# One level of Strassen in the second feed-forward product, on one core of Trainium2

The kernel runs on one core of a Trainium2 chip. The metric is the device time of one execution in microseconds. Every kernel below was run beside the kernel before on the same chip. All runs quoted are fast: none is over 1.5% above the fastest run of its kernel.

## The reference

Four batches go through linear attention and then through a feed-forward block behind a Fourier mixing. Cut to what matters:

```python
# q, k, v: (4, 8, 768, 64); w_ch1: (512, 2048); w_ch2: (2048, 512)
for t in range(S):                      # per head: decaying state
    state = gamma * state + outer(k[t], v[t])
    y[t] = scale * q[t] @ state
x = y as (4, 768, 512)
u = x + real(fft(fft(x, axis=1), axis=2))
un = (u - mean(u)) / sqrt(var(u) + 1e-6)           # per row of 512
out = u + maximum(un @ w_ch1, 0) @ w_ch2
```

Per batch, 768 rows of 512 go through two products, 512 to 2048 and 2048 to 512. The kernel multiplies in 16-bit floats and adds up in 32 bits.

## The kernel before

A scheduler merges streams of units by a position that each is given (`emit`). The main stream is the feed-forward work of batch b. The attention and the mixing of batch b+1 are mixed into it, so every engine has one queue in which both kinds of work alternate, and it works through this queue in order.

```python
inp = pool("inp", 11)                      # buffers for q, k, v in 32 bits
ps_g = pool("ps_g", 5, space=PSUM)         # attention and mixing
ps_pm = pool("ps_pm", 3, space=PSUM)       # the two feed-forward products

def h_unit(b, rt, fb):                     # first product, 384 rows, 128 hidden columns
    psh = ps_pm.tile([P, 384], ...)
    for cb in range(4):
        nc.tensor.matmul(psh, w116[:, cb, fb*P:(fb+1)*P], unT[:, cb, rt*384:(rt+1)*384], ...)
    if fb in ACT_ROWS[...]:                # 8 to 10 of 16 on ScalarE
        nc.scalar.activation(ht16[:, fb, :], psh, AF.Relu, bias=0.0, scale=-1.0)
    else:                                  # the others on VectorE
        nc.vector.tensor_scalar(out=ht16[:, fb, :], in0=psh, scalar1=-1.0, scalar2=0.0,
                                op0=ALU.mult, op1=ALU.max)

def ch_unit(b, rt, rb3, part):             # second product, 128 rows, in 4 parts
    # ... a PSUM tile psc of 512 columns
    for fb in range(k0, k0 + NFB // n):
        nc.tensor.matmul(psc[:, c0:c1], ht16[:, fb, rb3*P:(rb3+1)*P], w216[:, fb, c0:c1], ...)
    if part % n == n - 1:
        nc.vector.scalar_tensor_tensor(out=ob[:, c0:c1], in0=psc[:, c0:c1], scalar=r,
                                       in1=u[:, rb, c0:c1], op0=ALU.mult, op1=ALU.add)
        nc.sync.dma_start(out[b, rb*P:(rb+1)*P, c0:c1], ob[:, c0:c1])
# ... batch 0 makes its first row tiles one at a time (h0_unit)
# feed-forward of a batch: 16 h_units, 3 x 4 ch_units, 16 h_units, 3 x 4 ch_units
```

## Time and profile before

| | before |
|---|---|
| time, median of 5 runs | 247.66 us (247.35 to 247.86) |
| span of the profiled run | 246.0 us |
| TensorE busy | 234.4 us |
| VectorE, ScalarE, GpSimd busy | 177.5, 124.3, 81.3 us |
| chain that ended last | 72% TensorE, 8% VectorE, 7% GpSimd |

Busy time says how long an engine had an instruction in work. The chain that ended last is the path from the last instruction back to the start, at each step to whatever released it. Here that path is nearly always TensorE's own previous instruction. The prediction shows the lines.

### The profile page before, as it was taken

How to read it: one execution, taken by the hardware profiler on the slowest of the kernel's cores; microseconds unless marked ns; L12 is line 12 of the kernel's file. 1: busy time of each engine (PE TensorE's matmuls, PEld its weight loads, DVE VectorE, ACT ScalarE, POOL GpSimd, SP SyncE). 2: the span in 40 equal slices, each digit the busy share in tenths (PEclk: the TensorE clock that was granted, in tenths of full speed). 3: DMA queues.
4: the chain of work that ended last, by engine and by line, in shares of the span. 5: the costliest groups of instructions: out<-in, count | busy, mean ns of one | idle time of the engine just before them, and what ended most of it. 6: DMA issues, size and time to landing. Idle time of an engine off the chain costs nothing.

```text
span 246.0 us, 5309 instructions
## 1 busy us (share of the span) xinstructions
PE 234.4 (95%) x2024; PEld 144.4 (59%) x2024; DVE 177.5 (72%) x430; ACT 124.3 (51%) x276; POOL 81.3 (33%) x146
## 2 busy tenths in 40 slices
PE   6897899999999999999999999999999998999994
PEld 2454668956676655665567446665666455445543
DVE  8998957898788788995987648887895657424122
ACT  8798669477785445742247415732257217202500
POOL 6667600376500068690001637660003214000000
PEclk9999999999999999999999999999999999999999
DMA  8998999699999287988999589596100331121012
GB/s 174 257 260 138 200 204 206 152 250 261 275 233 214 56 171 176 190 174 149 242 266 210 119 183 181 108 138 150 58 0 3 60 133 30 38 85 43 0 45 85
DMA packets 99209, 36.39 MB, mean 148 GB/s; under 512 B 89840, under 2 KB 96240, under 8 KB 99184
## 3 DMA queue, kind: packets, MB, share of 16 engines
q1 hardware_dynamic: 94960, 31.86, 62.5%
q0 software_dynamic: 4224, 4.19, 10.5%
q8 instruction: 16, 0.26, 0.5%
q14 instruction: 9, 0.07, 0.1%
HBM read 27.26 MB, written 6.29 MB: 136 GB/s over the span
## 4 chain that ended last, share of the span: by engine, by line
PE 72%; DVE 8%; POOL 7%; ACT 4%; SPq 3%; DMA 2%; issue 2%; POOLq 0%; DVEq 0%
PE psc L973 30%; PE psh L930 23%; SPq L159 3%; PE ps L730 3%; PE psh L947 3%; PE wkA L594 3%; DMA k<-in_k_dram 2%; PE wkY L648 2%; POOL u L864 2%; POOL u L866 2%; PE wkY L644 1%; DVE bst L883 1%; PE wkK L613 1%; DVE u L834 1%; PE pq L827 1%
## 5 line engine op out<-in xcount | busy, mean ns | idle before, releaser
L973 PE MATMUL psc<-w,ht 128*128 128x512 f16 (+1 forms) x400 | 89.6, 370 | 0.1
L930 PE MATMUL psh<-unT,w 128*128 128x384 f16 x448 | 81.3, 326 | 0.6 <-ACT ht L934 0.6
L973 PEld LDWEIGHTS <-ht 128*128 128x128 f16 x400 | 38.1, 98 | 35.5 <-issue 0.3
L930 PEld LDWEIGHTS <-w 128*128 128x128 f16 x448 | 42.3, 98 | 24.9 <-issue 1.3
L934 ACT ACTIVATE ht<-psh 128x384 f16<-128x384 f32 x64 | 30.6, 488 | 39.4 <-PE psh L930 38.3
L864 POOL TENSOR_TENSOR u<-u,x 128x256 f32<-128x256 f32 x21 | 13.3, 634 | 102.3 <-DVE u L834 90.7
L977 DVE SCALAR_TENSOR_TENSOR ob<-psc,stats,u 128x512 f32<-128x512 f32 (+1 forms) x25 | 18.1, 722 | 27.4 <-PE psc L973 27.3
L936 DVE TENSOR_SCALAR ht<-psh 128x384 f16<-128x384 f32 x48 | 26.3, 551 | 8.6 <-PE psh L930 8.3
L597 DVE TENSOR_TENSOR atm<-wkA,maskp 128x512 f16<-128x512 f32 x36 | 23.9, 685 | 1.0 <-PE wkA L594 1.0
L885 ACT ACTIVATE un<-u,stats 128x512 f16<-128x512 f32 x21 | 15.1, 721 | 16.9 <-DVE stats L884 8.7
L883 DVE BATCH_NORM_STATS2 bst<-u 128x6 f32<-128x512 f32 x21 | 14.6, 694 | 9.7 <-POOL u L866 9.5
L623 DVE SCALAR_TENSOR_TENSOR s<-s,gk,wkK 128x128 f16<-128x128 f16 x48 | 16.4, 343 | 2.3 <-ACT s L619 1.4
L656 ACT ACTIVATE x<-wkY,gexp 128x384 f16<-128x384 f32 x24 | 12.8, 580 | 9.3 <-PE wkY L648 9.3
L145 PE MATMUL wps<-ht 128*128 128x512 f16 x40 | 13.3, 439 | 2.2 <-POOL ht L196 2.2
L377 POOL TENSOR_SCALAR kd<-k,gexp 128x384 f16<-128x384 f32 x24 | 13.8, 584 | 2.4 <-DMA k<-in_k_dram 2.4
L866 POOL TENSOR_TENSOR u<-u,x 128x256 f32<-128x256 f32 x21 | 13.3, 634 | 2.8 <-DVE u L837 1.5
L594 PE MATMUL wkA<-qTz,kT 128*128 128x256 f16 x72 | 13.6, 273 | 0.0
L829 ACT COPY qn<-pq 128x128 f32<-128x128 f32 x18 | 4.9, 274 | 14.1 <-PE pq L827 13.9
L947 PE MATMUL psh<-unT,w 128*128 128x128 f16 x192 | 11.5, 219 | 0.1
L947 PEld LDWEIGHTS <-w 128*128 128x128 f16 x192 | 11.0, 98 | 0.7 <-issue 0.5
L382 POOL TENSOR_SCALAR v<-v 128x768 f16<-128x768 f32 x12 | 10.0, 830 | 2.0 <-DMA v<-in_v_dram 1.9
L594 PEld LDWEIGHTS <-kT 128*128 128x128 f16 x72 | 6.9, 98 | 6.0 <-DVE s L623 0.4
(164 smaller groups left out, 318.2 us busy)
## 6 DMA issues: line engine op xcount, KB each, us to landing
q<-in_q_dram SPq DMA_DIRECT2D x16, 384.0 KB, 6.2
k<-in_k_dram SPq DMA_DIRECT2D x16, 384.0 KB, 5.6
v<-in_v_dram SPq DMA_DIRECT2D x16, 384.0 KB, 6.6
out_dram<-ob SPq DMA_DIRECT2D x23, 256.0 KB, 2.6
w<-in_moe_w_ch_dram POOLq DMA_DIRECT2D x8, 512.0 KB, 11.1
out_dram<-ob SPq DMA_DIRECT2D x2, 128.0 KB, 1.7
unT<-un SPq DMA_TRANSPOSE x15, 2.4
qTz<-q16z SPq DMA_TRANSPOSE x8, 3.8
```

The lines of the kernel that those rows point to most:

```text
L594: mm = nc.tensor.matmul(wk[:, c2], st["kT"][:, c, :], st["qT"][:, :, c, :], start=True, stop=True)
L597: nc.vector.tensor_tensor(out=st["atm"][:, 2 * part:2 * part + 2], in0=wk, in1=maskp[:, PAIR_ORDER[i]].unsqueeze(1).to_broadcast([P, 2, 2, ...
L623: nc.vector.scalar_tensor_tensor(out=s16[:, c], in0=s16[:, c - 1], scalar=gk2[:, hp:hp + 1], in1=wk[:, c - c0], op0=ALU.mult, op1=ALU.add)
L864: nc.gpsimd.tensor_tensor(out=u[:, kb, 0:256], in0=u[:, kb, 0:256], in1=x[:, kb, 0, 1:257], op=ALU.add)
L866: nc.gpsimd.tensor_tensor(out=u[:, kb, 256:512], in0=u[:, kb, 256:512], in1=x[:, kb, 1, 257:1:-1], op=ALU.add)
L883: nc.vector.bn_stats(bst, u[:, kb, :])
L930: nc.tensor.matmul(psh, w116[:, cb, fb * P:(fb + 1) * P], unT[:, cb, rt * 384:(rt + 1) * 384], start=(cb == 0), stop=(cb == 3))
L934: nc.scalar.activation(ht16[:, fb, :], psh, AF.Relu, bias=0.0, scale=-1.0)
L936: nc.vector.tensor_scalar(out=ht16[:, fb, :], in0=psh, scalar1=-1.0, scalar2=0.0, op0=ALU.mult, op1=ALU.max)
L947: mm = nc.tensor.matmul(psh[:, f], w116[:, cb, fb * P:(fb + 1) * P], unT[:, cb, kb * P:(kb + 1) * P], start=(cb == 0), stop=(cb == 3))
L973: nc.tensor.matmul(psc[:, c0:c1], ht16[:, fb, rb3 * P:(rb3 + 1) * P], w216[:, fb, c0:c1], start=(fb == 0), stop=(fb == NFB - 1))
L977: nc.vector.scalar_tensor_tensor(out=ob[:, c0:c1], in0=psc[:, c0:c1], scalar=lb[b]["st"][:, rb, 3:4], in1=lb[b]["u"][:, rb, c0:c1], op0=AL ...
```

## The change

Strassen's method computes a product of 2x2 blocks with seven block products in place of eight, and pays with sums of blocks. A group is 256 rows: two row tiles of 128 and two halves of the 2048 hidden columns. The weights are cut into two halves of hidden rows and two of output columns. So one group takes 7 x 8 matmuls of 256 columns in place of 2 x 16 of 512. The input sums are four adds of 512 elements per half group on VectorE, the weight differences eight VectorE operations once, and the seven results are combined by ScalarE copies, GpSimd adds and VectorE adds into `u`, from which the output is stored. To make room, the input buffers go from 11 to 7. All ReLUs of the new row groups run on ScalarE. The diff cut to its core:

```diff
-    inp = pool("inp", 11)
+    inp = pool("inp", 7)
...
-            psh = ps_pm.tile([P, 384], f32, tag="pm", name="psh", padded_shape=[P, DM])
...
-            if fb in ACT_ROWS[2 if (b, rt) == (B - 1, 0) else rt]:
-                nc.scalar.activation(ht16[:, fb, :], psh, AF.Relu, bias=0.0, scale=-1.0)
+            psh = ps_pm.tile([P, 2, 2 * P], f32, tag="pm", name="psh")
...
+            nc.scalar.activation(ht16[:, :, j, :], psh, AF.Relu, bias=0.0, scale=-1.0)
+
+    def sa_unit(c):
...
+            nc.vector.tensor_tensor(out=x1, in0=a21, in1=a22, op=ALU.add)
+            nc.vector.tensor_tensor(out=x2, in0=x1, in1=a11, op=ALU.subtract)
+            nc.vector.tensor_tensor(out=x4, in0=a12, in1=x2, op=ALU.subtract)
+            nc.vector.tensor_tensor(out=x3, in0=a11, in1=a21, op=ALU.subtract)
...
+    def sw_unit(n, c):          # weight differences, in batch 0
...
+    def p_unit(b, g, n):        # product n of group g
...
+                1: (ht16[:, 0, :, t1], w216[:, 0:NH, lo], "a", 0),
+                4: (ht16[:, 1, :, t2_], sw[:, 2], "a", 1),
+                2: (ht16[:, 1, :, t1], w216[:, NH:, lo], "b", 0),
+                5: (sa[:, 0], sw[:, 0], "b", 1),
+                6: (sa[:, 1], sw[:, 1], "a", 0),
+                3: (sa[:, 3], w216[:, NH:, hi], "b", 1),
+                7: (sa[:, 2], w216[:, 0:NH, hi], "a", 0),
...
+            if n == 1:
+                nc.scalar.activation(e1, ps, AF.Copy, bias=0.0, scale=r1)
+            elif n == 4:
+                add(k2, lo, r2)
+            elif n == 2:
+                add(k1, lo, r1)
+                nc.gpsimd.tensor_tensor(out=u[:, k1, lo], in0=u[:, k1, lo], in1=e1, op=ALU.add)
...
+            elif n == 5:
+                nc.scalar.activation(e5, ps, AF.Copy, bias=0.0, scale=r2)
...
+            un = [p_unit(b, g, n) for n in (1, 4, 2, 5, 6, 3, 7)]
+            un[0] = both(un[0], sa_unit(1))
```

The letters "a" and "b" are two PSUM tiles of two halves each, in which products are added on top of one another (6 and 7 on 1, 3 on 5). Batch 0 keeps the ordinary product for its first four row tiles, so 10 groups of 256 rows take the new way.

More of the change, by code (lines that the diff above doesn't have):

```diff
@@ L33 @@
 NPE = 2
-ACT_ROWS = ((2, 5, 6, 7, 8, 9, 10, 14), (0, 3, 6, 7, 9, 10, 11, 12, 14, 15), (2, 4, 5, 6, 7, 8, 10, 14))
+NH = NFB // 2
+HM = DM // 2
 @with_exitstack
@@ L67 @@
     hp_ = pool("hp", 1)
-    obp = pool("obp", 3)
     stt = pool("stt", 2)
@@ L88 @@
     gk5 = const.tile([P, NHP, D, NCH - 1], f32, tag="gk5")
+    gkf = gk5.rearrange("p n e c -> p (n e c)")
+    e1, e5 = gkf[:, 320:320 + HM], gkf[:, 320 + HM:320 + 2 * HM]
     t2 = gk5[:, 0].rearrange("p e c -> p (e c)").bitcast(f16)[:, 0:520].rearrange(
@@ L135, in held @@
         return run
-    ht16 = hp_.tile([P, NFB, 384], f16, tag="ht16")
-    wz = ht16[:, 0:2, :].rearrange("p a b -> p (a b)")[:, 0:DM]
+    ht16 = hp_.tile([P, 2, NH, 2 * P], f16, tag="ht16")
+    sw = const.tile([P, 3, NH, HM], f16, tag="sw")
+    sa = const.tile([P, 4, NH, P], f16, tag="sa")
+    spare = sw.rearrange("p n j m -> p (n j m)").bitcast(f32)
+    wz = ht16[:, 0, 0:2, :].rearrange("p a b -> p (a b)")
     wps = ps_w.tile([P, DM], f32, tag="w", name="wps")
@@ L154, in run @@
             h0 = 2 * PAIR_ORDER[i]
-            for name, src in srcs.items():
-                t = inp.tile([P, 2, NCH, D], f32, tag="in32", name=f"{name}32")
+            for n, (name, src) in enumerate(srcs.items()):
+                if b == 0 and 7 <= 3 * i + n < 11:
+                    w = NCH * P
+                    t = spare[:, (3 * i + n - 7) * w:(3 * i + n - 6) * w].rearrange(
+                        "p (h c d) -> p h c d", h=2, c=NCH)
+                else:
+                    t = inp.tile([P, 2, NCH, D], f32, tag="in32", name=f"{name}32")
                 rows = "h (p c) d -> p h c d" if b < NPE and name == "q" else \
@@ L187 @@
     kf = tmp[:, 1, 0:KN]
+    ht0 = tmp2.rearrange("p a b -> p (a b)").bitcast(f16).rearrange("p (f t) -> p f t", f=NFB)
     rs = [tmp[:, 2 + n] if n < 4 else tmp2[:, n - 4] for n in range(10)]
@@ L890, in norm_unit, with rstd_unit @@
         return run
-    def rstd_unit(b, rt):
+    def rstd_unit(b, k0, k1):
         def run():
             stats = lb[b]["st"]
-            if b == 0 and rt == 0:
-                for kb in range(3):
+            if b == 0 and k0 == 0:
+                for kb in range(k1):
                     bst = lb[0].pop(("bst", kb))
@@ L899, in run @@
                     nc.vector.bn_aggr(stats[:, kb, 0:2], bst)
-            sl = slice(3 * rt, 3 * rt + 3)
-            nc.scalar.activation(stats[:, sl, 2:3], stats[:, sl, 1:2], AF.Sqrt, bias=epsT,
+            nc.scalar.activation(stats[:, k0:k1, 2:3], stats[:, k0:k1, 1:2], AF.Sqrt, bias=epsT,
                                  scale=1.0)
-            nc.vector.reciprocal(out=stats[:, sl, 3:4], in_=stats[:, sl, 2:3])
+            nc.vector.reciprocal(out=stats[:, k0:k1, 3:4], in_=stats[:, k0:k1, 2:3])
         return run
@@ L922, in unT_unit, with h_unit @@
         return run
-    def h_unit(b, rt, fb):
+    def h_unit(b, g, j):
         def run():
             unT = lb[b]["unT"]
-            psh = ps_pm.tile([P, 384], f32, tag="pm", name="psh", padded_shape=[P, DM])
-            for cb in range(4):
-                nc.tensor.matmul(psh, w116[:, cb, fb * P:(fb + 1) * P],
-                                 unT[:, cb, rt * 384:(rt + 1) * 384],
-                                 start=(cb == 0), stop=(cb == 3))
-            if fb in ACT_ROWS[2 if (b, rt) == (B - 1, 0) else rt]:
-                nc.scalar.activation(ht16[:, fb, :], psh, AF.Relu, bias=0.0, scale=-1.0)
-            else:
-                nc.vector.tensor_scalar(out=ht16[:, fb, :], in0=psh, scalar1=-1.0, scalar2=0.0,
-                                        op0=ALU.mult, op1=ALU.max)
+            psh = ps_pm.tile([P, 2, 2 * P], f32, tag="pm", name="psh")
+            for h in range(2):
+                fb = NH * h + j
+                for cb in range(4):
+                    nc.tensor.matmul(psh[:, h], w116[:, cb, fb * P:(fb + 1) * P],
+                                     unT[:, cb, 2 * P * g:2 * P * (g + 1)],
+                                     start=(cb == 0), stop=(cb == 3))
+            nc.scalar.activation(ht16[:, :, j, :], psh, AF.Relu, bias=0.0, scale=-1.0)
+        return run
@@ new lines, in sa_unit, with run @@
+    def sa_unit(c):
+        def run():
+            js = slice(4 * c, 4 * c + 4)
+            a11, a12 = (ht16[:, n, js, 0:P] for n in range(2))
+            a21, a22 = (ht16[:, n, js, P:2 * P] for n in range(2))
+            x1, x2, x3, x4 = (sa[:, n, js, :] for n in range(4))
+            nc.vector.tensor_tensor(out=x1, in0=a21, in1=a22, op=ALU.add)
+            nc.vector.tensor_tensor(out=x2, in0=x1, in1=a11, op=ALU.subtract)
+            nc.vector.tensor_tensor(out=x4, in0=a12, in1=x2, op=ALU.subtract)
+            nc.vector.tensor_tensor(out=x3, in0=a11, in1=a21, op=ALU.subtract)
+        return run
@@ new lines, in sw_unit, with run @@
+    def sw_unit(n, c):
+        def run():
+            js = slice(4 * c, 4 * c + 4)
+            b11, b12 = w216[:, js, 0:HM], w216[:, js, HM:DM]
+            ks = slice(NH + 4 * c, NH + 4 * c + 4)
+            b21, b22 = w216[:, ks, 0:HM], w216[:, ks, HM:DM]
+            t1, t2_, t4 = (sw[:, m, js, :] for m in range(3))
+            dst, x, y = ((t1, b12, b11), (t2_, b22, t1), (t4, b21, t2_), (b12, b22, b12))[n]
+            nc.vector.tensor_tensor(out=dst, in0=x, in1=y, op=ALU.subtract)
+        return run
@@ new lines, with run, add, put @@
+    pr = {}
+    def p_unit(b, g, n):
+        def run():
+            tail = b == B - 1 and g == 2
+            u, st = lb[b]["u"], lb[b]["st"]
+            k1, k2 = 2 * g, 2 * g + 1
+            r1, r2 = st[:, k1, 3:4], st[:, k2, 3:4]
+            t1, t2_ = slice(0, P), slice(P, 2 * P)
+            lo, hi = slice(0, HM), slice(HM, DM)
+            if n == 1:
+                pr["a"] = ps_pm.tile([P, 2, HM], f32, tag="pm", name="pra")
+            elif n == 2:
+                pr["b"] = ps_pm.tile([P, 2, HM], f32, tag="pm", name="prb")
+            lhs, rhs, key, half = {
+                1: (ht16[:, 0, :, t1], w216[:, 0:NH, lo], "a", 0),
[5 more added lines that the diff above has]
+                7: (sa[:, 2], w216[:, 0:NH, hi], "a", 0),
+            }[n]
+            ps = pr[key][:, half]
+            for j in range(NH):
+                nc.tensor.matmul(ps, lhs[:, j], rhs[:, j], start=(n in (1, 2) and j == 0),
+                                 stop=(n in (2, 3, 4, 7) and j == NH - 1), skip_group_check=True)
+            def add(k, cs, r, src=ps):
+                nc.vector.scalar_tensor_tensor(out=u[:, k, cs], in0=src, scalar=r,
+                                               in1=u[:, k, cs], op0=ALU.mult, op1=ALU.add)
+            def put(k, cs=slice(0, DM)):
+                nc.sync.dma_start(out[b, k * P:(k + 1) * P, cs], u[:, k, cs])
+            if n == 1:
+                nc.scalar.activation(e1, ps, AF.Copy, bias=0.0, scale=r1)
+            elif n == 4:
+                add(k2, lo, r2)
+            elif n == 2:
+                add(k1, lo, r1)
+                nc.gpsimd.tensor_tensor(out=u[:, k1, lo], in0=u[:, k1, lo], in1=e1, op=ALU.add)
+                if tail:
+                    put(k1, lo)
+            elif n == 5:
+                nc.scalar.activation(e5, ps, AF.Copy, bias=0.0, scale=r2)
+            elif n == 6:
+                add(k1, hi, r1)
+                if tail:
+                    nc.gpsimd.tensor_tensor(out=u[:, k2, hi], in0=u[:, k2, hi], in1=e5,
+                                            op=ALU.add)
+            elif n == 3:
+                add(k1, hi, r1)
+                put(k1, hi if tail else slice(0, DM))
+            else:
+                if tail:
+                    for cs in (lo, hi):
+                        add(k2, cs, r2)
+                        put(k2, cs)
+                else:
+                    nc.vector.scalar_tensor_tensor(
+                        out=u[:, k2].rearrange("p (a m) -> p a m", a=2),
+                        in0=ps.unsqueeze(1).to_broadcast([P, 2, HM]), scalar=r2,
+                        in1=u[:, k2].rearrange("p (a m) -> p a m", a=2), op0=ALU.mult,
+                        op1=ALU.add)
+                    nc.gpsimd.tensor_tensor(out=u[:, k2, hi], in0=u[:, k2, hi], in1=e5,
+                                            op=ALU.add)
+                    put(k2)
@@ L951, in run @@
                 lb[0]["mm"] = mm
-            dst = ht16[:, 4 * g:4 * g + 4, kb * P:(kb + 1) * P]
+            dst = ht0[:, 4 * g:4 * g + 4, kb % 3 * P:(kb % 3 + 1) * P]
             if g % 2 == 0:
@@ L960, with ch_unit @@
     psc_of = {}
-    def ch_unit(b, rt, rb3, part):
+    def ch_unit(rb, part):
         def run():
-            rb = rt * 3 + rb3
-            split = b == B - 1 and rb == NCH - 1
-            n = 2 if split else 4
-            if part % n == 0:
+            if part == 0:
                 psc_of[0] = ps_pm.tile([P, DM], f32, tag="pm", name="psc")
-            psc = psc_of[0]
-            c0, c1 = (256 * (part // 2), 256 * (part // 2) + 256) if split else (0, DM)
-            k0 = NFB // n * (part % n)
-            for fb in range(k0, k0 + NFB // n):
-                nc.tensor.matmul(psc[:, c0:c1], ht16[:, fb, rb3 * P:(rb3 + 1) * P],
-                                 w216[:, fb, c0:c1], start=(fb == 0), stop=(fb == NFB - 1))
-            if part % n == n - 1:
-                ob = obp.tile([P, DM], f32, tag="ob", name="ob")
-                nc.vector.scalar_tensor_tensor(out=ob[:, c0:c1], in0=psc[:, c0:c1],
-                                               scalar=lb[b]["st"][:, rb, 3:4],
-                                               in1=lb[b]["u"][:, rb, c0:c1], op0=ALU.mult,
-                                               op1=ALU.add)
-                nc.sync.dma_start(out[b, rb * P:(rb + 1) * P, c0:c1], ob[:, c0:c1])
+            psc, u = psc_of[0], lb[0]["u"]
+            for fb in range(4 * part, 4 * part + 4):
+                nc.tensor.matmul(psc, ht0[:, fb, rb % 3 * P:(rb % 3 + 1) * P], w216[:, fb, :],
+                                 start=(fb == 0), stop=(fb == NFB - 1))
+            if part == 3:
+                nc.vector.scalar_tensor_tensor(out=u[:, rb, :], in0=psc,
+                                               scalar=lb[0]["st"][:, rb, 3:4], in1=u[:, rb, :],
+                                               op0=ALU.mult, op1=ALU.add)
+                nc.sync.dma_start(out[0, rb * P:(rb + 1) * P, :], u[:, rb, :])
         return run
@@ L1084, in mix_units, with both, run @@
         return [s2_unit(b, kb) for kb in kbs], [unT_unit(b, kb) for kb in kbs]
+    def both(*units):
+        def run():
+            for u in units:
+                u()
+        return run
     def emit(streams):
@@ L1108, with h_tiles, products @@
         majors = []
+        def h_tiles(g):
+            un = [h_unit(b, g, j) for j in range(NH)]
+            un[1] = both(un[1], rstd_unit(b, 2 * g, 2 * g + 2))
+            un[5] = both(un[5], sa_unit(0))
+            return un
+        def products(g):
+            un = [p_unit(b, g, n) for n in (1, 4, 2, 5, 6, 3, 7)]
+            un[0] = both(un[0], sa_unit(1))
+            return un
         if b == 0:
@@ L1113 @@
                 majors += [h0_unit(kb, g) for g in range(4)]
-        else:
-            majors += [h_unit(b, 0, fb) for fb in range(NFB)]
-        majors.append(rstd_unit(b, 0))
-        majors += [ch_unit(b, 0, rb3, part) for rb3 in range(3) for part in range(4)]
-        majors += [h_unit(b, 1, fb) for fb in range(NFB)]
-        majors.append(rstd_unit(b, 1))
-        majors += [ch_unit(b, 1, rb3, part) for rb3 in range(3) for part in range(4)]
+            majors[-1] = both(majors[-1], rstd_unit(0, 0, 3))
+            ch = [[ch_unit(rb, part) for part in range(4)] for rb in range(4)]
+            for rb, n in ((1, 0), (2, 1), (3, 2)):
+                for c in range(2):
+                    ch[rb][2 * c] = both(ch[rb][2 * c], sw_unit(n, c))
+            majors += ch[0] + ch[1] + ch[2]
+            majors += [h0_unit(3, g) for g in range(4)] + [rstd_unit(0, 3, 4)] + ch[3]
+            un = h_tiles(2)
+            for c in range(2):
+                un[2 + c] = both(un[2 + c], sw_unit(3, c))
+            majors += un + products(2)
+        else:
+            for g in range(3):
+                majors += h_tiles(g) + products(g)
         s2s, unTs = mix_units(b, [3, 4, 5])
```

## The prediction

> **What bounds the kernel now.** I first read the page's busy times and its costliest groups. TensorE is the only engine close to full.
>
> ```profile
> span 246.0 us, 5309 instructions
> PE 234.4 (95%) x2024; PEld 144.4 (59%) x2024; DVE 177.5 (72%) x430; ACT 124.3 (51%) x276; POOL 81.3 (33%) x146
> ...
> L973 PE MATMUL psc<-w,ht 128*128 128x512 f16 (+1 forms) x400 | 89.6, 370 | 0.1
> L930 PE MATMUL psh<-unT,w 128*128 128x384 f16 x448 | 81.3, 326 | 0.6 <-ACT ht L934 0.6
> L934 ACT ACTIVATE ht<-psh 128x384 f16<-128x384 f32 x64 | 30.6, 488 | 39.4 <-PE psh L930 38.3
> L977 DVE SCALAR_TENSOR_TENSOR ob<-psc,stats,u 128x512 f32<-128x512 f32 (+1 forms) x25 | 18.1, 722 | 27.4 <-PE psc L973 27.3
> L936 DVE TENSOR_SCALAR ht<-psh 128x384 f16<-128x384 f32 x48 | 26.3, 551 | 8.6 <-PE psh L930 8.3
> ```
>
> L930 is the first feed-forward product, L973 the second, and TensorE waits for almost nothing before either. The means of 370 and 326 ns are durations of overlapping matmuls, not their pace. The pace comes from the chain that ended last, where a run of matmuls is merged into start, length and count:
>
> ```profile
> 74.34 0.44 PE wkA L594 x4
> ...
> 189.03 10.36 PE psc L973 x48
> ...
> 222.02 10.40 PE psh L930 x64
> 232.42 10.41 PE psc L973 x64
> 242.86 0.48 DVE ob L977
> ```
>
> So 512 columns take 10.36/48 = 215.8 ns, 384 take 162.5 ns and 256 (wkA is 128x256) 110 ns. The last 64 are 32 of 512 and 32 of 256 columns: 32 x 215.8 + 32 x 109.2 = 10.4 us, so 109.2 ns for 256. In an earlier part of the same chain 112 matmuls of 128 columns (L947) took 6.40 us, 57.1 ns each. A weight load before every matmul limits none of these.
>
> Next I asked for the busy times by stage, cut where the chain passes from one batch's feed-forward work to the next:
>
> ```profile
> 41.16:83.90 42.74, 42.52 (x467) 29.69 (x467) 36.56 (x93) 28.25 (x52) 14.81 (x22) 1.00 1.05 217
> 83.90:136.47 52.57, 52.05 (x441) 32.89 (x439) 43.00 (x105) 25.74 (x62) 20.14 (x34) 1.00 0.98 190
> 136.47:189.03 52.56, 52.16 (x414) 31.59 (x413) 40.13 (x97) 22.73 (x55) 18.88 (x32) 1.00 0.53 104
> 189.03:246.00 56.97, 53.09 (x300) 28.68 (x298) 22.87 (x48) 14.71 (x35) 6.14 (x10) 1.00 0.19 56
> ```
>
> The columns are length, then PE, weight loads, DVE, ACT and POOL with their counts. In the first three stages, each of which also holds the next batch's attention, TensorE is full and VectorE is at 119.7 of 147.9 us, 81%. In the last stage VectorE has room. The granted clock is full throughout.
>
> [...]
>
> [...] The trace has 553 ns for 768 elements (L673, L683) and 354 ns for 384, that is 0.52 ns per element, so 421 ns for 512 and 686 ns for 1024.
>
> [...]
>
> ```profile
> 53.81 0.82 POOL L367 TENSOR_SCALAR q16z<-q 128x768 f16<-128x768 f32 x1
> ...
> 53.84 0.88 DVE L244 TENSOR_SCALAR gk<-cd,last 128x128 f16<-128x128 f16 x1
> ...
> 55.16 0.27 DVE L248 TENSOR_SCALAR gk<-sd,last 128x128 f16<-128x128 f16 x1
> ```
>
> L244 and L248 have one shape, but the one that starts just behind a GpSimd cast lasts 0.88 instead of 0.27 us. The two-input adds of before (L683: 549 to 561 ns, all 16) fall on no cast; some of the new ones will.
>
> **The change, part by part.** *TensorE.* For 256 rows the second product was 2 x 16 matmuls of 512 columns; it becomes 7 x 8 of 256. The first product goes from 384 to 256 columns. Per batch 1 to 3: before 128 x 162.5 + 96 x 215.8 = 41.5 us; after (192 + 168) x 109.2 = 39.3 us, so -2.2. Batch 0 keeps four row tiles as they were: before 192 x 57.1 + 64 x 162.5 + 96 x 215.8 = 42.1; after 256 x 57.1 + 120 x 109.2 + 64 x 215.8 = 41.5, so -0.6. Sum: -0.6 - 3 x 2.2 = **-7.2 us**. One product in eight is saved, but it is half of the feed-forward work and in 10 of 12 row groups only[...]. This is all the change can win.
>
> *VectorE.* Its durations overlap: in 136.47 to 189.03 its groups add up to 46.5 us where it is busy 40.1 us with 97 instructions, so I take 66 ns off each. Per batch 1 to 3: 14 ReLUs leave, -14 x 0.484 = -6.8; 24 input sums come, 24 x 0.355 = +8.5; six output adds of 512 columns (0.745 each) become 12 of 256 (0.484, from the last row tile of before) and three of 512, 12 x 0.418 - 3 x 0.679 = +3.0; one reciprocal, +0.1. Net +4.8. Batch 0: six ReLUs leave (-2.9), two of L956 come (+1.2), eight input sums (+2.8), eight weight differences of 1024 (8 x 0.62 = +5.0), output adds +1.0; net +7.1. VectorE in the first three stages: 119.7 + 7.1 + 2 x 4.8 = 136.4 us, against 147.9 - 0.6 - 2 x 2.2 = 142.9 us of TensorE's work: **95% in place of 81%**[...].
>
> [...] GpSimd gets two adds per group (L864's 634 ns each) and is then busy about 24 of 50 us in a stage. If half of the 24 sums begin during a GpSimd instruction and wait half of one (0.3 us), this is about 3.5 us a stage and 2 us in batch 0, an estimate from these durations: 136.4 + 9 = 145.4 us, more than TensorE's 142.9.
>
> *ScalarE.* 64 ReLUs of 488 ns become 80 of 592 (L954's), +16.1; 20 scaled copies of 256 at 0.37 (L855's), +7.4; two more of L954, +1.2; four square roots of 0.29, +1.1. It is busy 150 of 246 us: not a bound. *Loads.* The seventh buffer first binds in batch 1, whose last five loads wait for casts that in the trace of before are done by about 56 us; those loads were issued between 54.4 and 60.1 us there[...]. I count nothing. *Outputs* in place save no time.
>
> **The rivals.** (a) TensorE stays the bound and the whole -7.2 us arrives, about 240.5 us. For it: 0.1 and 0.6 us of idle before L973 and L930; the built order of instructions fills gaps between products with the next group's first product. Against: VectorE at 95%. (b) VectorE becomes the bound of the first three stages. TensorE's order is fixed, so each late sum (fifth product) or late output add (frees the bank of the seventh) stops it. With 145.4 us of work and some idle around it, the stages take 148 to 150 us: nothing gained there, only 2 us in the last batch; 246 to 250 us. (c) Waits inside a group: two PSUM tiles carry seven products, so the sixth and third products wait for ScalarE copies, the seventh for a VectorE add made during one product of 0.87 us; the old tiles had 3.45 us and three buffers. At 0.2 to 0.5 us per group over 10 groups: +2 to +5, so 242.5 to 245.5 us. (d) Group 1 now needs row tile 3's normalised rows at 35% of the batch's sequence instead of 52%; the chain of before already shows this path as the last to arrive at 148 to 157 and 201 to 211 us, with about 0.4 us of TensorE lost each time. A later arrival costs 1 to 2 us a batch.
>
> **Range and chances.** I choose between (a) and (b) with some of (c): the first three stages shrink from 147.9 to about 146 us, because VectorE can push part of its backlog into the next batch and the compiler's order hides some sums behind GpSimd's idle times; the last stage wins 2.2 us and gives about 0.7 back at product boundaries and in the tail (two adds after the last product where there was one). Sum: -1.9 - 1.5 = -3.4, so 244.2 us. Low, 240.8: nearly all of (a). High, 249.0: (b) in full. 2% is 5.0 us, a gain of 70% of the ceiling of 7.2: I give it 0.28. Slower by over 2% (252.6) needs (b) and (d) together: 0.06. Within 2%: 0.66.
>
> **What would show it.** *Right:* matmuls of 256 columns at 109 ns in the chain, for 7.2 us less TensorE work; VectorE over 90% busy in the first three stages; its 512-element sums at 0.42 us with some at 0.7 to 1 us during GpSimd's casts; TensorE's idle, 0.9 us in the middle two stages together, rising to 1 to 2 us a stage and put down to VectorE. *Wrong:* if those stages come out at 143 us, VectorE's load was no obstacle and (a) holds; if idle before the products names ScalarE, or the casts wait for loads, it was the evacuations or the seven buffers; if 256-column products with a fresh weight load each pace above 115 ns, the gain itself was mis-sized.

## The result, and the profile after

| | before | after |
|---|---|---|
| time, median of 5 runs | 247.66 us | 274.75 us (274.56 to 276.7) |
| ratio | | 1.1114 (1.1083 to 1.1145) |

The result is correct, and the kernel is 27 us slower. Ratios are the mean time of one kernel's fast runs over that of the other's of the same rounds, so they differ slightly from the ratio of the medians. The profiled run of the changed kernel is the slowest of its five (276.7 us).

From the page of the changed kernel: span, busy times, TensorE's clock in 40 slices, the chain that ended last by engine, and groups of instructions (count, busy us and mean ns; then the engine's idle time before them and what ended it).

```profile
span 274.8 us, 6447 instructions
PE 239.3 (87%) x2504; PEld 191.4 (70%) x2504; DVE 204.9 (75%) x506; ACT 149.6 (54%) x318; POOL 101.3 (37%) x166
...
PEclk9999999998999979988999999988999999999999
...
PE 44%; DVE 29%; POOL 8%; ACT 7%; issue 5%; DMA 3%; SPq 3%; DVEq 0%; ACTq 0%; POOLq 0%
...
L942 PE MATMUL psh<-unT,w 128*128 128x256 f16 x640 | 79.7, 272 | 0.9 <-ACT ht L945 0.9
L945 ACT ACTIVATE ht<-psh 128x512 f16<-128x512 f32 x80 | 47.2, 596 | 37.3 <-PE psh L942 37.2
...
L996 PE MATMUL pra<-sw,sa 128*128 128x256 f16 x80 | 13.5, 299 | 6.7 <-DVE u L1000 6.5
...
L954 DVE TENSOR_TENSOR sa<-ht 128x512 f16<-128x512 f16 x20 | 8.3, 414 | 12.6 <-ACT ht L945 12.6
...
L996 PE MATMUL pra<-w,ht 128*128 128x256 f16 x80 | 11.5, 273 | 4.8 <-ACT ht L945 4.8
```

Before, 72% of the chain was TensorE and 8% VectorE; now it is 44% and 29%. TensorE is still the busiest engine, but it waits. Products (L996) wait for a VectorE add (L1000), then for a ReLU (L945); VectorE's first sum (L954) waits 12.6 us for ReLUs; ScalarE's ReLUs (L945) wait 37 us for TensorE, as they did before (38 us). Everyone waits for somebody.

I counted TensorE from 41 us on in both traces, from the start of one matmul to the start of the next. As work I took the pace of the chain before, 109.2, 162.5 and 215.8 ns for 256, 384 and 512 columns, and for other widths the straight line through these (29 and 56 ns for 64 and 128 columns, which is also the median from start to start in both traces); whatever goes beyond it is waiting.

| from 41 us to the last matmul | before | after | difference |
|---|---|---|---|
| work | 196.1 us | 188.7 us | -7.4 |
| waiting | 5.7 us | 40.8 us | +35.1 |

The gain came, and nearly five times as much went into waits. About 6.3 of the 40.8 us are matmuls at half clock, of which more below.

The last product of batches 0 to 2 ends at 199.22 us before and at 226.21 us after. Up to there the next batch's attention and mixing run beside the feed-forward work; behind it stands the last batch. Busy times of these two stretches, of the kernel before and of the changed one; the columns are length, PE, weight loads, DVE, ACT, POOL with counts, clock, and DMA (share and GB/s):

```profile
41.16:199.22 158.06, 156.92 (x1365) 98.74 (x1365) 124.60 (x304) 79.70 (x174) 56.28 (x92) 1.00 0.81 162
199.22:246.00 46.78, 42.90 (x253) 24.11 (x251) 17.96 (x35) 11.73 (x28) 3.68 (x6) 1.00 0.15 49
...
41.16:226.21 185.05, 163.15 (x1730) 134.58 (x1728) 147.31 (x360) 96.34 (x203) 70.84 (x105) 0.96 0.70 138
226.21:274.80 48.59, 41.80 (x370) 35.12 (x367) 22.89 (x55) 20.27 (x41) 8.96 (x13) 1.00 0.16 52
```

So 27.0 us of the loss arose in the first three batches, about evenly (10.3, 8.6 and 8.1 us), and 1.8 us in the last one. In the first three VectorE is busy 147.3 of 185.1 us, or 80%. Before, it was 124.6 of 158.1, or 79%. So it did not become full; the stretch grew with its work.

What TensorE waited for, from the view of waits (us in total, times, longest):

```profile
PE pra L996 <- DVE u L1000: 7.5, 8, 2.7
PE pra L996 <- ACT ht L945: 4.8, 5, 1.4
PE pst L924 <- ACT un L896: 3.1, 2, 1.7
PE wkA L605 <- DVE s L634: 2.2, 1, 2.2
```

No single wait explains 35 us. Counted from start to start, ten waits of over 1 us make 19.5 of the 40.8 us; the rest are small. A stretch of the timeline (start us, duration us; lines between are left out) shows how one such wait comes about; L954 to L957 are the input sums, L845 is an addition of the mixing on VectorE, L875 and L877 are GpSimd's adds of the mixing, and L894 to L896 normalise the rows.

```profile
215.56 0.63 POOL L875 TENSOR_TENSOR u<-u,x 128x256 f32<-128x256 f32 x1 [1.59 <-DVE u L845]
215.79 0.68 DVE L955 TENSOR_TENSOR sa<-sa,ht 128x512 f16<-128x512 f16 x1
216.15 0.82 POOL L877 TENSOR_TENSOR u<-u,x 128x256 f32<-128x256 f32 x1
216.40 0.85 DVE L957 TENSOR_TENSOR sa<-ht 128x512 f16<-128x512 f16 x1
217.18 0.68 DVE L894 BATCH_NORM_STATS2 bst<-u 128x6 f32<-128x512 f32 x1
217.78 0.46 DVE L845 SCALAR_TENSOR_TENSOR u<-pq,g,qn 128x256 f32<-128x256 f32 x1
218.16 0.17 DVE L895 BATCH_NORM_AGGREGATE stats<-bst 128x2 f32<-128x6 f32 x1
218.41 0.72 ACT L896 ACTIVATE un<-u,stats 128x512 f16<-128x512 f32 x1 [0.70 <-issue]
219.04 0.58 ACT L945 ACTIVATE ht<-psh 128x512 f16<-128x512 f32 x1
219.68 0.28 PE L996 MATMUL pra<-w,ht 128*128 128x256 f16 x1 [1.42 <-ACT ht L945]
```

L955 and L957 last 0.68 and 0.85 us; the same sums last 0.42 and 0.39 us at 221.10 and 220.79 us. Each ends 0.28 us after the GpSimd add that it overlaps (216.19 and 216.97). This is so in the whole trace: of the 80 sums, the 57 that begin outside GpSimd's instructions last 0.39 to 0.43 us; of the 23 that begin within one, 19 end 0.27 to 0.28 us after it, and the other four end before it, not stretched.

The row statistics (L894) need GpSimd's second add (L877), which lasts 0.82 us beside the sums and 0.64 us at 213.33 us, and they start 0.21 us after it, behind the last stretched sum. Their second part (L895) stands 0.30 us behind L845. `un` (L896) on ScalarE needs it. ScalarE is idle for 0.70 us before `un`, although the matmuls for the group's last ReLU (L945) had ended at 217.48 us: the ReLU stands behind `un` in the queue. The last matmul of the first product needs that ReLU. TensorE loses 1.42 us to a delay that came through GpSimd, VectorE and ScalarE in turn; the stretched sums are the smaller part of it.

The last thing is TensorE's clock. In the profiled run of the changed kernel it was at half speed four times, 3.41 us each time, from 60.84, 98.39, 122.28 and 183.72 us. (The mean clock of this run is 0.975; the 0.981 of the other four would fit three such windows, an estimate.) The chain shows it (start us, us, what), eight matmuls of 256 columns at full speed taking 0.87 us:

```profile
99.25 1.71 PE pra L996 x8
...
122.61 1.71 PE prb L996 x8
...
126.14 0.87 PE prb L996 x8
```

Each half-speed window can cost at most half its length, so 6.8 us in all is a bound. The four starts are whole multiples of 3.413 us apart (11, 7 and 18 times). I laid that grid over this trace and took TensorE's share of work in each window. The shares ahead of the four were 0.29, 0.07, 0.15 and 0.32; of the whole windows from 41 us to the last matmul, the lowest that was not followed by half speed had 0.48. So in this trace the slow clock comes after waiting: it is a further price of it, not its origin.

### The profile page after: what moved, and what is told of

Its sections match the earlier page's. It is cut to its first block, busy times and chain, and to the rows that moved or that the text cites.

```text
span 274.8 us, 6447 instructions
## 1 busy us (share of the span) xinstructions
PE 239.3 (87%) x2504; PEld 191.4 (70%) x2504; DVE 204.9 (75%) x506; ACT 149.6 (54%) x318; POOL 101.3 (37%) x166
## 4 chain that ended last, share of the span: by engine, by line
PE 44%; DVE 29%; POOL 8%; ACT 7%; issue 5%; DMA 3%; SPq 3%; DVEq 0%; ACTq 0%; POOLq 0%
PE psh L942 12%; PE pra L996 9%; PE prb L996 8%; DVE bst L894 3%; PE ps L741 3%; SPq L169 3%; POOL u L877 3%; ACT ht L945 3%; DVE atm L608 3%; PE psc L1069 2%; DVE eo L694 2%; PE wkA L605 2%; DVE xab L684 2%; DVE s L634 2%; POOL u L875 2%
## 5 line engine op out<-in xcount | busy, mean ns | idle before, releaser
L942 PE MATMUL psh<-unT,w 128*128 128x256 f16 x640 | 79.7, 272 | 0.9 <-ACT ht L945 0.9
L945 ACT ACTIVATE ht<-psh 128x512 f16<-128x512 f32 x80 | 47.2, 596 | 37.3 <-PE psh L942 37.2
L996 PEld LDWEIGHTS <-sa 128*128 128x128 f16 x320 | 32.7, 103 | 14.7 <-issue 9.7
L875 POOL TENSOR_TENSOR u<-u,x 128x256 f32<-128x256 f32 x21 | 13.7, 651 | 60.6 <-DVE u L845 49.9
L996 PEld LDWEIGHTS <-ht 128*128 128x128 f16 x240 | 22.6, 98 | 10.3 <-ACT ht L945 6.7
L1012 POOL TENSOR_TENSOR u<-u,gk 128x256 f32<-128x256 f32 x10 | 7.6, 763 | 56.1 <-DVE u L1000 49.3
L896 ACT ACTIVATE un<-u,stats 128x512 f16<-128x512 f32 x21 | 15.2, 722 | 16.9 <-DVE stats L895 12.1
L894 DVE BATCH_NORM_STATS2 bst<-u 128x6 f32<-128x512 f32 x21 | 14.5, 692 | 9.8 <-POOL u L877 9.7
L996 PE MATMUL pra<-sw,sa 128*128 128x256 f16 x80 | 13.5, 299 | 6.7 <-DVE u L1000 6.5
L1069 PE MATMUL psc<-w,tmp 128*128 128x512 f16 x64 | 17.7, 399 | 0.7 <-DVE tmp L1057 0.7
L954 DVE TENSOR_TENSOR sa<-ht 128x512 f16<-128x512 f16 x20 | 8.3, 414 | 12.6 <-ACT ht L945 12.6
L1000 DVE SCALAR_TENSOR_TENSOR u<-pra,stats,u 128x256 f32<-128x256 f32 x22 | 10.4, 478 | 9.4 <-PE pra L996 9.4
L1036 POOL TENSOR_TENSOR u<-u,gk 128x256 f32<-128x256 f32 x9 | 6.5, 727 | 28.8 <-DVE u L1031 25.1
L996 PE MATMUL pra<-w,ht 128*128 128x256 f16 x80 | 11.5, 273 | 4.8 <-ACT ht L945 4.8
L877 POOL TENSOR_TENSOR u<-u,x 128x256 f32<-128x256 f32 x21 | 14.8, 705 | 1.9 <-DVE u L869 1.3
```

The costliest lines, as they stand in the source:

```text
L875: nc.gpsimd.tensor_tensor(out=u[:, kb, 0:256], in0=u[:, kb, 0:256], in1=x[:, kb, 0, 1:257], op=ALU.add)
L877: nc.gpsimd.tensor_tensor(out=u[:, kb, 256:512], in0=u[:, kb, 256:512], in1=x[:, kb, 1, 257:1:-1], op=ALU.add)
L894: nc.vector.bn_stats(bst, u[:, kb, :])
L942: nc.tensor.matmul(psh[:, h], w116[:, cb, fb * P:(fb + 1) * P], unT[:, cb, 2 * P * g:2 * P * (g + 1)], start=(cb == 0), stop=(cb == 3))
L945: nc.scalar.activation(ht16[:, :, j, :], psh, AF.Relu, bias=0.0, scale=-1.0)
L996: nc.tensor.matmul(ps, lhs[:, j], rhs[:, j], start=(n in (1, 2) and j == 0), stop=(n in (2, 3, 4, 7) and j == NH - 1), skip_group_check=True)
```

## The experiments

The kernels differ from the kernel before or from the changed one by the edits shown. Those called "wrong" give a wrong result so that a piece of work can be taken away. The expectations call a theory by a letter: A is the relay, in which each product waits for the results of the sums and adds before it; A' is the order of the instructions in the queues; C is what the change does outside Strassen's products (256-row groups, ReLUs, buffers, output in place); E is the queue of ReLUs on ScalarE; F is the place of the mixing in the sequence. The load theory says that the sheer amount of work in the in-order queues of VectorE, ScalarE and GpSimd costs, wherever it stands.

### plain2: the changed kernel with an ordinary second product

```diff
-            un = [p_unit(b, g, n) for n in (1, 4, 2, 5, 6, 3, 7)]
+            return [q_unit(b, 2 * g + rt, part) for rt in range(2) for part in range(4)]
-            un[5] = both(un[5], sa_unit(0))      # and no weight differences
```

> The changed kernel with its second product as ordinary matmuls (2 x 16 of 512 columns per 256 rows, one output add per row tile), no sums, no weight differences; 256-row groups, all later ReLUs on ScalarE, residual in place and 7 buffers stay. Theory A (the relay: seven products share two PSUM banks, so every product waits for the previous reading of its bank by VectorE or ScalarE, with only some 0.2 us of slack each) and theory B (the input sums load VectorE and its queue): 246 to 252 us, TensorE's waiting back near 6 to 10 us. Theory C (the accompanying changes do it: ReLUs behind other work in ScalarE's queue, 7 buffers, 256-row groups): 262 us or more.

256.35 us, ratio 1.0351 (1.0321 to 1.0382), correct. One third of the loss, 8.7 us, is there without any Strassen. TensorE waits about 13 us, counted as above.

### no_sa: no input sums (wrong)

```diff
-                5: (sa[:, 0], sw[:, 0], "b", 1),
-                6: (sa[:, 1], sw[:, 1], "a", 0),
+                5: (ht16[:, 0, :, t2_], sw[:, 0], "b", 1),
+                6: (ht16[:, 0, :, t1], sw[:, 1], "a", 0),
...
-            un[5] = both(un[5], sa_unit(0))
-            un[0] = both(un[0], sa_unit(1))
```

> The changed kernel without the 80 input sums; products 5, 6, 3, 7 read the activations themselves, so the result is wrong on purpose and all matmuls and output adds stay. A: still 264 us or more, for the relay stays; VectorE falls by about 30 us. B: 256 us or less. C: 268 us or more.

268.01 us, 1.0822. The 80 sums cost 6.7 us of 27.

### sa_unused: the sums are made and not read (wrong)

The products read `ht16` as in no_sa, while `sa_unit` stays.

> As the last, but the sums are computed and nothing reads them (wrong on purpose): VectorE's load without TensorE's wait for the sums. If the load of the sums costs the time: as the changed kernel, 270 us or more. If the wait for their result does: as the kernel without sums. A and C: between 264 and 275 us and little different from the kernel without sums.

275.78 us, 1.1136: as slow as the changed kernel. So on balance no time is lost by waiting for the sums' results; making the sums is what costs. This took theory A's first half away.

### banks4 and psum35: four PSUM tiles for the products, and its control

```diff
-    ps_g = pool("ps_g", 5, space=PSUM)
+    ps_g = pool("ps_g", 3, space=PSUM)
-    ps_pm = pool("ps_pm", 3, space=PSUM)
+    ps_pm = pool("ps_pm", 5, space=PSUM)
# banks4 only: products 4 and 5 get tiles of their own
+                4: (ht16[:, 1, :, t2_], sw[:, 2], "c", 0),
+                5: (sa[:, 0], sw[:, 0], "d", 0),
```

> The changed kernel with four PSUM banks for the products in place of two (products 1, 6, 7 in one, 4, 2, and 5 with 3 in one each), 5 banks for the feed-forward part and 3 for the rest in place of 3 and 5 (a control with only that follows). A: 262 us or less, waits at the products gone. B, C: 270 us or more.

> The control for the four product banks: the changed kernel with 3 PSUM banks for attention and mixing and 5 for the feed-forward part, products still in two banks. If taking two banks from the attention hid a gain of the four product banks, this is 280 us or more and the four banks are worth the difference to 273.9. If the sharing of banks never mattered, it is within 2 us of 273.9.

banks4: 273.86 us, 1.1058 (1.0989 to 1.1127), correct. psum35: 280.69 us, 1.1334, correct. With the buffers split 3 to 5, own tiles for the products are worth 6.8 us; but taking two buffers from the attention and mixing costs 5.9 us (psum35 against the changed kernel). Sharing two tiles is a part of the loss, and this split of the eight buffers does not buy it off; other splits were not tried.

### bare: no sums, no copies, no small adds (wrong)

From no_sa, the ScalarE copies, GpSimd adds and small VectorE adds go; two VectorE adds of 512 per 256 rows remain, as in the kernel before.

> Seven products and nothing around them (wrong on purpose): no input sums, no ScalarE copies, no GpSimd adds, and as in the kernel with ordinary products two output adds of 512 columns per 256 rows, when all products of their bank are done. Theory D (the products' many small readings between them cost the 12 us that lie between the kernel with ordinary products, 256.4, and the kernel without sums, 268.0): TensorE's 7 us arrive and it is 248 to 252 us. If instead 256-column products with a weight load each, or their order, cost the time: 262 us or more.

257.96 us, 1.0416. The seven products with hardly more side work than before are still 10 us slower than the kernel before.

### plain2_split: half of the ReLUs back to VectorE

```diff
-            nc.scalar.activation(ht16[:, :, j, :], psh, AF.Relu, bias=0.0, scale=-1.0)
+            if j in (0, 2, 5, 7):
+                nc.scalar.activation(ht16[:, :, j, :], psh, AF.Relu, bias=0.0, scale=-1.0)
+            else:
+                nc.vector.tensor_scalar(out=ht16[:, :, j, :], in0=psh, scalar1=-1.0, ...)
```

> The kernel with ordinary second products, but half of the later ReLUs (tiles 1, 3, 4, 6 of 8) on VectorE as before. Theory E (the 8.7 us that this kernel lost come from the ReLUs standing behind other work in one queue, ScalarE's): 249 to 252 us. If they come from the 7 buffers, the 256-row groups or the order: 255 us or more.

256.53 us, 1.0358, correct, against plain2's 256.35. In this setting it makes no difference which engine has the ReLUs.

### inp7: the kernel before with seven input buffers

```diff
-    inp = pool("inp", 11)
+    inp = pool("inp", 7)
+    spare = const.tile([P, 4 * NCH * P], f32, tag="spare")   # loads 8 to 11 of batch 0
```

> The kernel before with only the 7 input buffers (and a spare place for the four loads of batch 0, as the change has). If the buffers alone delay loads or the transposes behind them in the queue: 250 us or more. If they are harmless, as predicted: 247 to 248.5 us.

252.32 us, 1.0188 (1.0159 to 1.0218), correct: 4.6 us for the four buffers alone, under 2% but clear of noise. In its waits, TensorE's attention products (L600) wait for data that was there in time before; neither of these two lines is among the first seven of the kernel before:

```profile
PE wkA L600 <- DMA kT<-kd: 2.8, 2, 1.8
...
PE wkA L600 <- ACT x L662: 1.6, 1, 1.6
```

Counted from start to start, these three waits, at 117, 155 and 164 us, are 4.9 us, about the whole loss. The two for `kT` end with DMA transposes that land at 155.3 and 164.0 us; in the kernel before, the same two land at 149.7 and 156.3 us. They are issued from SyncE's queue, in which the loads stand too, and the third wait is for ScalarE, which had itself waited for such a transpose. This fits loads that wait for a free buffer and hold up what stands behind them; it was not tested apart.

### overlap, overlap_late, late_mix, bare_late: moving work in the sequence

```diff
# overlap: four products of a group go among the next group's first-product tiles
-            un = [p_unit(b, g, n) for n in (1, 4, 2, 5, 6, 3, 7)]
+            un = [p_unit(b, g, n) for n in (1, 4, 2)]
+            carry[:] = [p_unit(b, g, n) for n in (5, 6, 3, 7)]
# late: the mixing of row tiles 3 to 5 gets more room
-        dm = ... (0.004, 0.140, 0.232, 0.341)
+        dm = ... (0.004, 0.420, 0.100, 0.510)
```

> The changed kernel in another order: only products 1, 4 and 2 follow their group's first product at once; 5, 6, 3 and 7 stand between the next group's first-product tiles, so that each reading of a bank has a tile's 0.87 us more and the sums have 2.6 us of products and 0.9 us of a tile before them. Theory A' (it is the reaction time between products that costs, in whatever queue): 262 us or less. If the amount of work on VectorE and ScalarE costs, not its place: 270 us or more.

> The last, and the mixing of row tiles 3 to 5 spread over the first 42% of a batch in place of the first 14%. Theory F (normalisation work stands ahead of the ReLUs and sums in the in-order queues just when the first group of a batch ends): 4 us or more below the last. Otherwise within 2 us of it.

> The changed kernel with only that later mixing. F: 268 us or less, the waits of product 1 for the last ReLU (5.6 us in all) mostly gone. Otherwise 273 us or more.

> The seven bare products (258.0; wrong on purpose) with only that later mixing. F: 252 us or less, so that some of TensorE's 7 us show at last. Otherwise 256 us or more.

| kernel | us | ratio |
|---|---|---|
| overlap (correct) | 275.58 | 1.1119 |
| overlap_late (correct) | 276.1 | 1.114 |
| late_mix (correct) | 275.7 | 1.1124 |
| bare_late (wrong) | 260.48 | 1.051 |

None helps, and the last is 2.5 us worse than bare. Giving TensorE other work between a result and its use hardly changed the sum of the waits, so order (A') and place (F) fell as explanations, as far as these orders go.

### ideal: bare without weight differences and with 11 buffers (wrong)

> The seven bare products (wrong on purpose) without the weight differences either, and with 11 buffers as before; only 256-row groups, ReLUs on ScalarE and the residual in place are left of the rest. If TensorE's saving can arrive when nothing is laid on the other engines: 241 to 246 us. If another chain of waits takes its place at once: 248 us or more.

251.0 us, 1.013 (1.0101 to 1.016). Buffers and weight differences are worth 7.0 us together. But even here TensorE's 7.3 us of saved work is not to be seen.

### no_e: no_sa without the ScalarE copies and GpSimd adds (wrong)

```diff
-                nc.scalar.activation(e1, ps, AF.Copy, bias=0.0, scale=r1)
-                nc.gpsimd.tensor_tensor(out=u[:, k1, lo], in0=u[:, k1, lo], in1=e1, op=ALU.add)
-                nc.scalar.activation(e5, ps, AF.Copy, bias=0.0, scale=r2)
-                    nc.gpsimd.tensor_tensor(out=u[:, k2, hi], in0=u[:, k2, hi], in1=e5, ...)
```

> The kernel without sums (268.0; wrong on purpose) and without the 20 ScalarE copies and 19 GpSimd adds of products 1 and 5; the small VectorE adds stay. If copies and GpSimd adds make the 10 us above the bare products: 258 to 261 us. If the small adds of VectorE do: 265 us or more.

261.07 us, 1.0536. Against no_sa, 20 copies and 19 GpSimd adds cost 6.9 us; against bare, the small VectorE adds cost 3.1 us. Whether the copies or the GpSimd adds weigh more was not separated.

### bare_sums: bare with the 80 sums, unread (wrong)

> The bare products (258.0; wrong on purpose) with the 80 input sums computed and not read: their load alone. If the sums cost the same in any surroundings: 264 to 267 us. If their load only hurts together with the small adds: 261 us or less.

262.62 us, 1.0599: +4.7 us on bare, where the same sums cost 6.7 us between no_sa and the changed kernel and 7.8 between no_sa and sa_unused. The costs nearly add up, a little more than so where the queues are fuller.

### before_sums: the kernel before with 84 unread sums

```diff
+            if fb % 4 == 3:
+                for n in range(3):
+                    nc.vector.tensor_tensor(out=junk_sa, in0=ht16[:, fb - 3:fb + 1, ...],
+                                            in1=ht16[:, fb - 3:fb + 1, ...], op=ALU.add)
```

> The kernel before with 84 sums of the same form and size (512 16-bit elements, read from the activations) written to a place that nobody reads; 12 per half batch. If VectorE had room, as the 81% seem to say: 247.7 to 250 us. If the old kernel's order leaves no room on VectorE for 30 us of such work: 254 us or more.

257.87 us, 1.0407 (1.0377 to 1.0437), correct, with the clock at full speed throughout. From its page, its groups on VectorE by shape, and the two stretches as above (first three batches, last batch):

```profile
PE 237.4 (93%) x2024; PEld 144.0 (56%) x2024; DVE 206.0 (80%) x514; ACT 124.4 (49%) x276; POOL 85.1 (33%) x146
...
L940 DVE TENSOR_TENSOR gk<-ht 128x512 f16<-128x512 f16 x84 | 37.7, 448 | 3.8 <-ACT ht L934 3.5
...
41.16:208.74 167.58, 159.62 (x1365) 98.18 (x1364) 145.06 (x364) 79.93 (x174) 59.39 (x92) 1.00 0.74 153
208.74:256.20 47.46, 43.17 (x253) 24.10 (x251) 26.30 (x59) 11.62 (x28) 4.27 (x6) 1.00 0.15 48
```

This is the load theory's cleanest test: VectorE's busy time is 206.0 us, as in the changed kernel (204.9), nothing else is changed, no product reads the sums, and 10.1 us are lost. VectorE has 50 us of idle time in this trace all the same. Where the work fell made the difference. In the first three batches 20.5 us more of VectorE's time took 9.5 us, and its share rose from 79% to 87%: the idle fifth was room for about half of the work. In the last batch, where VectorE had been 38% busy, 8.3 us more took 0.7 us. The run does not part the amount of work from its place: the sums stand behind the ReLUs that they read (3.8 us of idle time before them), and some last up to 0.79 us (the mean is 448 ns), where the sums outside GpSimd's instructions took 0.39 to 0.43 us in the changed kernel.

### ideal_order and after_order: more work between the last ReLU and its use

In ideal, counted from start to start, 7.7 of TensorE's 15.2 us of waiting were the first product's wait for the group's last ReLU: that product asks for it after 0.76 us of matmuls, and the ReLU itself lasts 0.6 us. The old second product asked after 15 matmuls of 512 columns, 3.2 us.

```diff
+            if n == 1:
+                for j in range(NH - 1):
+                    mm(ps, lhs, rhs, n, j)
+                for j in range(NH - 1):
+                    mm(pr["a"][:, 1], ht16[:, 1, :, t2_], sw[:, 2], 4, j)
+                mm(ps, lhs, rhs, n, NH - 1)
+                mm(pr["a"][:, 1], ht16[:, 1, :, t2_], sw[:, 2], 4, NH - 1)
```

> The kernel 'ideal' (251.0 us; wrong result on purpose; its TensorE work from 41 us on is 188.8 us and its waits 15.2) with one change of order: the last two matmuls of products 1 and 4, which alone need the group's last ReLU, stand behind the first fourteen of both, so that TensorE has 1.6 us instead of 0.8 us of work in front of them. In 'ideal' the waits of product 1 for ScalarE's ReLU sum to 7.7 of the 15.2 us. Theory 'product 1 follows too close behind the last ReLU' (what is left in 'ideal'): the five waits of 1.0 to 1.9 us each lose up to 0.8 us, 3.5 to 5 us in all, so 246 to 247.5 us, level with the kernel before. Load theory in its strict form (a wait taken away comes back at another place): 250 to 251 us.

> The changed kernel (274.8 us, correct result) with the same change of order. There product 1 waits 5.6 us for ScalarE's ReLU, and other waits, above all that of product 6 for VectorE's adds (9.4 us), are larger. If the place of the last ReLU were a cause of its own: 270 to 272 us. Load theory: VectorE, ScalarE and GpSimd keep their work and order, so the time stays within 2 us of 274.8, with less waiting of product 1 for ScalarE and more at product 6, which now follows product 4's add with less work between (product 4 ends at the same time, product 1's copy 0.8 us later).

ideal_order (wrong): 248.3 us, 1.0028 (1.0014 to 1.0042). after_order: 273.36 us, 1.1032 (1.1005 to 1.1058), correct. In the view of waits, which counts idle time only, of ideal:

```profile
PE pra L993 <- ACT ht L942: 6.7, 6, 1.7
```

of ideal_order:

```profile
PE pra L993 <- ACT ht L942: 3.4, 5, 1.0
```

and of after_order:

```profile
PE pra L996 <- DVE u L1011: 10.3, 8, 3.1
...
PE pra L996 <- ACT ht L945: 1.8, 3, 0.7
```

In ideal, 3.3 us less waiting for the ReLU gave 2.7 us of time, a little less than the 3.5 to 5 us expected. That closeness was a cause of its own there. In the changed kernel the same edit took 3.0 us off the wait for the ReLU (4.8 to 1.8) and put 2.8 us on the wait for VectorE's add (7.5 to 10.3); 1.4 us were won. This fits a longer chain of work on the other engines that arrives at the same time anyway.

### The sum

Each step of this ladder was measured; another order of steps would split the same 27 us somewhat differently.

| step | us | added |
|---|---|---|
| before | 247.7 | |
| 256-row groups, seven bare products, ReLUs on ScalarE, output in place (ideal) | 251.0 | +3.3 |
| seven buffers and weight differences (bare) | 258.0 | +7.0 |
| small VectorE adds (no_e) | 261.1 | +3.1 |
| ScalarE copies and GpSimd adds (no_sa) | 268.0 | +6.9 |
| input sums (after) | 274.8 | +6.7 |

The first step contains the gain of about 7.3 us, so the new grouping costs some 10 us of waits, of which ideal_order won back 2.7 with a few lines. What holds the rest of that step was not settled. The half-speed windows number four in the changed kernel and one in bare (mean clocks 0.975 and 0.992), so at most three times 1.7, or 5.1 us, of the 16.8 us between these two can be the clock; the other steps contain some of it too. No kernel was faster than the kernel before.

## Why the prediction was wrong

Predicted 244.2 us with 249.0 as the upper end; it was 274.75.

**The gain on TensorE was right.** -7.2 us predicted, -7.4 measured, and 256 columns kept the pace of 109 ns with a fresh weight load each (the median from start to start in the changed kernel's trace).

**The load on VectorE was about right, and what it does was wrong.** To the first three batches the prediction added 7.1 + 2 x 4.8 = 16.7 us of VectorE work, plus 9 us for sums that begin beside GpSimd's instructions; measured were 22.7 us (124.6 to 147.3 us), the stretched sums included. (Its stages are cut at the wrong place: at 136.47 and 189.03 us the last products of a batch only begin; they end at 146.66 and 199.22 us. This changes VectorE's share before from 81% to 79%.) The step that failed is rival (b)'s "With 145.4 us of work and some idle around it, the stages take 148 to 150 us", at most about 2 us more than before, and the "VectorE over 90% busy" that was to show it. The first three batches take 27.0 us more, and VectorE is 80% busy, nearly as before. The prediction took VectorE's idle fifth for room that new instructions could use free of charge until it was full. before_sums shows that it was not: at that share, added work cost about half of its length. At this price VectorE's 22.7 us would be some 10.5 us of the 27 (an estimate from 9.5 for 20.5); the ladder's two VectorE steps, small adds and input sums, measured 9.8. The explanation that I give is that VectorE's idle time lies where it waits for TensorE, ScalarE or GpSimd, and work put into its queue delays what stands behind it, for which those engines wait in turn. That this happens through loops of in-order queues is what the stretch at 215 to 219 us shows in one instance; for the other waits I infer it from the load runs, and did not trace them one by one.

**The last batch did not win.** The prediction had "the last stage wins 2.2 us and gives about 0.7 back"; it lost 1.8 us, with VectorE 47% busy. TensorE's waiting in it rose from 1.3 to 4.9 us, counted from start to start. In no_sa, without the sums, it is 4.4 us, and in bare, without the copies and small adds too, 2.1 us: most of it comes with the readings between the products, which is rival (c)'s kind.

**"Loads ... I count nothing" was wrong.** The seven buffers alone cost the kernel before 4.6 us (inp7). The prediction looked at when the five loads of batch 1 are issued; it did not ask when the attention needs the data afterwards, and the waits came at 117 to 164 us.

**Rival (c), waits inside a group, was seen and mis-sized.** "At 0.2 to 0.5 us per group over 10 groups: +2 to +5". The products' waits for VectorE's adds and for ReLUs alone are 12.3 us in the view of waits, 4.8 of them put down to ScalarE, which the prediction had named as a sign of being wrong. The wait that the prediction missed is the first product's for the last ReLU, with 0.76 us in front of it where there had been 3.2. The sums that it took for the danger ("each late sum") were not waited for to any extent: sa_unused is as slow.

**ScalarE and GpSimd were set aside by their share.** "It is busy 150 of 246 us: not a bound." It was busy 149.6 us. Yet the copies and GpSimd adds cost 6.9 us. Single durations were also a little low: copies 474 ns where 370 was taken, GpSimd adds 763 and 727 ns where 634 was, four of the eight weight differences 0.98 to 1.30 us where 0.69 was. These are small beside the rest.

**The clock was not thought of.** The prediction had it at full speed; four windows at half speed cost up to 6.8 us.

The chances followed from the same step: with VectorE taken as free up to 95%, the worst case could only be VectorE's full length, and over 252.6 us got 0.06.

## What to carry to other kernels

In a kernel whose engines hand work around in in-order queues, an engine's idle share alone does not say how much room it has: to price added work, put that much dummy work into the kernel as it is, time it, and look at each stretch (the unread sums cost 9.5 us here where VectorE was 79% busy, and 0.7 us where it was 38% busy). Cut the stretches of two kernels at the same piece of work before comparing them. When a change saves work on the bounding engine and pays on the others, compare the saving with that price, and count for each new product how much work lies between the last result that it needs and the matmul that needs it. Buffers taken away to make room should be timed alone before the change is judged.
